# Attention and an eight-expert MoE on one core: the source of the clearing zeros, three chunks of expert 0, and expert 1's sums of x

## The chip, the cores and the metric

The kernel runs on one core of one Trainium2 chip. The metric is the device time of one execution in microseconds; the three timed runs of the kernel before gave 689.43, 690.41 and 692.71 us, with a median of 690.41 us. The engines are named as the profile names them: PE (TensorE; PEld is its weight load), DVE (VectorE), ACT (ScalarE), POOL (GpSimd) and SP (SyncE, which here only issues DMA transfers; SPq is its queue).

## The reference

Attention over 4 batches, 8 heads, 768 positions and 64 columns per head: each query sees the 31 keys within 16 positions and 24 block summaries (the maximum of 32 keys, the mean of 32 values). Its output, 3072 rows of 512, goes through a mixture of 8 experts; each row goes to the two with the highest noisy logits.

```python
x = np.ascontiguousarray(attn_out.transpose(0, 2, 1, 3)).reshape(B * S, H * D)   # 3072 x 512
logits = x @ w_gate
noise_scale = np.log1p(np.exp(x @ w_noise))
noisy_logits = logits + noise_scale * noise
top2 = np.argpartition(-noisy_logits, 2, axis=1)[:, :2]
...
for e in range(E):                      # 8
    for k in range(2):
        mask = top2[:, k] == e
        h = np.maximum(x[mask] @ w1[e], 0.0)                          # 512 -> 1024
        out[mask] += top2_w[mask, k, None] * (h @ w2[e])              # 1024 -> 512
```

## The kernel before

**Stages.** Attention runs over 24 row tiles of 128 rows and fills the first 145 us or so. Each finished tile of x is split into a high and a low half of fp16 (1024 columns together) and stored to a table `xd` in HBM; the gate is worked out beside it. A decoded table then holds, for every expert, the rows that it takes, in 816 slots: seven chunks, six of 128 rows and a last one of 48. The order of all instructions on each engine is that of the code (a manual schedule), so a waiting instruction holds up everything behind it on its engine.

**An expert's input.** `x_gather(e, c)` (L740) gathers the rows of a chunk from `xd` by an indirect DMA, issued on POOL, into one of four buffers `XG` taken in turn; the first three chunks of expert 1 go into the buffers `PREV` instead, which later hold earlier output rows. `x_trans(e, c)` (L754) transposes a chunk into `XTE[e]` by a DMA issued on SP (L758). `x_trans_pe` (L762) does the same by eight transposes on PE (L766) into a PSUM bank and one ACT copy out of it (L767); before, chunks 5 and 6 of expert 0 take that way.

**Weights.** `w_load(e, i)` (L621 for the four slices of w1, L624 for those of w2) brings a slice through one of four staging buffers `stg`; ACT and DVE split it into a high and a low half of fp16 (`w1_hi` L674, `w1_lo` L679, `w_hi`, `w_lo` L646). For experts 1 to 7 sums of blocks of w1 are made as well (`w1_sums`, DVE, L657 to L662).

**Expert 0's first layer** is plain: `mm1_pe` (L780), twelve matmuls for each of eight strips, in two halves. Half 0 is chunks 0 to 2, half 1 is chunks 3 to 6 and begins behind the second layer of chunks 0 to 2 (`mm2_high`, `mm2_low`, L931), between whose low passes the transposes on PE stand. `mm1_out` evicts a strip (ACT L790, DVE L791), and `y_out` scales a chunk's output on DVE (L952) and scatters it from POOL.

**Experts 1 to 7** use seven block products instead of eight for each of four strips, so 28 products (`mm1_all`, `product`, L816). Three of the x blocks and one of their combinations are sums: `t_diff` (POOL, L693) makes a difference of the high or of the low halves, `t_join` (DVE, L649) adds the two, and `t_two`, `t_four` (DVE), `t_hi` (ACT, L713) and `t_lo` (DVE, L649) make the four blocks and split them into fp16 (`tx`). `p` is an ACT copy of a product (L838), `c` a sum on DVE (L858), `htl` the low half of an evicted strip (L824).

**What sets the order.** For the preparation of expert e + 1 a table gives each step a tick within expert e: `put(e, k, f, ...)` and `steps` fill it, `step(e, k)` issues it. For experts 1 to 7 a tick is one product of the first layer (28 of them, `M2`) or one pass of the second (21). For expert 0 ticks 0 to 2 stand behind the low passes of chunks 0 to 2, ticks 3 to 10 behind the eight strips of half 1, the rest behind the passes of chunks 3 to 6. Ahead of that, `finish_table` (L1216) issues the gathers and loads that follow the gate. `clear` (L988) writes zeros to 384 rows of the output; it runs eight times, with the zeros read from `XG[3]`.

Of the kernel before, what the change touches and what calls it, by code (L numbers as in the profile page):

```python
# [8 lines left out]
F32 = mybir.dt.float32  # L9
# [5 lines left out]
OP = mybir.AluOpType  # L15
# [45 lines left out]
def attn_moe(ctx, tc, qt, kt, vt, wgn, noise, w1, w2, out):  # L61
    nc = tc.nc
# [32 lines left out]
    LAST = NCH - 1  # L95
# [180 lines left out]
    def bank():  # L276
        return banks[0].tile([P, 1, 512], F32, name="h")
# [339 lines left out]
    def w_load(e, i):  # L617
        s = stage.tile([P, SW], F32, name="stg")[:, :1024]
        SG[e, i] = s
        if i < 4:  # L620
            nc.sync.dma_start(s, w1[e, i * P:(i + 1) * P, :])  # L621
        else:
            i -= 4
            nc.sync.dma_start(s.rearrange("p (c d) -> p c d", c=2),  # L624
                              w2[e, 2 * i * P:2 * (i + 1) * P, :].rearrange("(c p) d -> p c d", p=P))
# [17 lines left out]
    def w_lo(e, i):  # L643
        n, sc = ("w1", W1S) if i < 4 else ("w2", W2S)
        hi, lo = [WT[e][n + x][:, i % 4, :] for x in "hl"]
        nc.vector.scalar_tensor_tensor(lo, SG[e, i], sc, hi, op0=OP.mult, op1=OP.subtract)  # L646

    def plus(o, a, b, op=OP.add):
        nc.vector.scalar_tensor_tensor(o, a, 1.0, b, op0=OP.mult, op1=op)  # L649
# [33 lines left out]
    def tt(e, j):  # L683
        TT[e, j] = side_pool[0].tile([P, 2, HC], F32, name=f"t{j}")
        return TT[e, j]

    def xb(e, j, k, low):
        return XTE[e][:, 4 * low + 2 * j:4 * low + 2 * j + 2, HC * k:HC * k + HC]

    def t_diff(e, j, low):  # L690
        i = (1, 1) if j == 3 else (0, 1)
        o = (0, 1) if j == 3 else (0, 0)
        nc.gpsimd.tensor_tensor(tt(e, 0 if low else j), xb(e, *i, low), xb(e, *o, low), op=OP.subtract)  # L693

    def t_join(e, j):
        plus(TT[e, j], TT[e, j], TT[e, 0])

# [56 lines left out]
    def x_trans(e, c):  # L754
        if c == 0:
            XTE[e] = (late[0] if e % 2 else moe).tile([P, 2 * DC, CAP], F16, name="xte")
        n = min(P, CAP - c * P)
        nc.sync.dma_start_transpose(out=XTE[e][:, :, c * P:c * P + n], in_=XC[e, c][:n])  # L758
# [3 lines left out]
    def x_trans_pe(e, c):  # L762
        n = min(P, CAP - c * P)
        pt = bank()[:, 0].bitcast(F16).rearrange("p (k n) -> p k n", k=2 * DC)
        for k in range(2 * DC):
            nc.tensor.transpose(pt[:, k, :n], XC[e, c][:n, k * P:(k + 1) * P], identh[:n, :n])  # L766
        nc.scalar.activation(XTE[e][:, :, c * P:c * P + n], pt[:, :, :n], AF.Copy)  # L767
# [18 lines left out]
    def mm1_out(e, half, f):  # L786
        c0, c1 = (0, H0) if half == 0 else (H0, CAP)
        ph = PH[f][:, :c1 - c0]
        hh, hl = HT
        nc.scalar.activation(hh[:, f, c0:c1], ph, AF.Relu)  # L790
        nc.vector.scalar_tensor_tensor(hl[:, f, c0:c1], ph, 0.0, hh[:, f, c0:c1], op0=OP.max, op1=OP.subtract)  # L791
# [149 lines left out]
    def mm2_low(e, c, pv):  # L941
        py = PY[c]
        mm2_pass(e, c, "w2l", HT[0], 2, py)
        y_out(e, c, pv)
# [197 lines left out]
    PREV = []  # L1142
    w1_alloc(1, True)
    for i in range(3):
        x = late[0].tile([P, DM], F32, name=f"prev{i}")
        PREV.append(x)

    spair.close()
# [24 lines left out]
    norm_lo(NT - 1, nc.vector)  # L1173
    x_out(NT - 1)
    for i in range(8):
        clear(XG[3].bitcast(F32), 3)
    for x in HT:
        nc.gpsimd.memset(x[:, :, CAP:], 0.0)
    for x in PREV:
        nc.gpsimd.memset(x, 0.0)  # L1180
    mm1_out(0, 0, 0)
    mm1_pe(0, 0, 1)
    mm1_pe(0, 0, 2, None, lambda: gate_c(5, og))
# [32 lines left out]
    def finish_table():  # L1216
        decode(TB.rearrange("p e c w -> p (e c) w"), 0, NS)
        last_ids()
        for c in range(3, NCH):
            x_gather(0, c)  # L1220
        for f in range(4, 8):
            w_lo(0, f)
        for c in range(3):
            x_gather(1, c)
        w_load(1, 0)
        w_load(1, 2)
        for c in range(3, LAST - 1):
            x_trans(0, c)
        w_load(1, 1)
        w_load(1, 3)  # L1230
        for c in range(3):
            x_trans(1, c)

    finish_table()
    mm2_high(0, 0)
# [10 lines left out]
    def put(e, k, f, *a):  # L1246
        plan.setdefault((e, k), []).append((f, a))
# [5 lines left out]
    def steps(e, where, at_):  # L1253
        for k, f, *a in at_:
            put(where, k, f, e, *a)

    for k, c in ((0, 3), (1, 4), (1, 5), (2, 6)):
        put(0, k, x_gather, 1, c)
        put(0, k, x_trans, 1, c)
    steps(1, 0, (  # L1260
        (1, w1_sums, 0, 0), (2, w1_sums, 0, 1), (2, w1_hi, 0, 0), (3, w1_lo, 0, 0), (3, w1_hi, 0, 1),
        (4, w1_lo, 0, 1, (0,)), (5, w1_lo, 0, 1, (1,)), (5, w1_sums, 1, 0), (6, w1_sums, 1, 1), (6, w1_hi, 1, 0),
        (7, w1_lo, 1, 0), (7, w1_hi, 1, 1), (8, w1_lo, 1, 1, (0,)), (8, t_diff, 3, 0), (8, t_diff, 3, 1),
        (9, w1_lo, 1, 1, (1,)), (9, t_diff, 1, 0), (11, t_join, 3), (11, t_diff, 1, 1), (11, t_alloc), (11, t_two, 0),
        (11, t_hi, 3), (12, t_two, 1), (12, t_hi, 2), (13, t_join, 1), (13, t_hi, 1), (14, t_lo, 3), (14, t_lo, 2),
        (15, t_four), (15, t_hi, 4), (16, t_lo, 1), (17, t_lo, 4)))
    for i, k in enumerate((13, 14, 18, 19)):
        put(0, k, w_load, 1, 4 + i)
    M2 = 7 * (FC // 2)

    def gathers(e, where, early, k):
        for c in range(4):
            put(where, early[c], x_gather, e, c)
            put(where, k, x_trans, e, c)
        for c in range(4, NCH):
            put(where, k + 2 * (c - 2), x_gather, e, c)
            put(where, k + 2 * (c - 2), x_trans, e, c)

    gathers(2, 0, (10, 10, 11, 11), 11)
    for e in range(1, E):  # L1280
        put(e, 0, w2_alloc, e)
        for i, (k0, k1) in enumerate(((3, 3), (8, 9), (15, 16), (22, 22))):
            put(e, k0, w_hi, e, 4 + i)
            put(e, k1, w_lo, e, 4 + i)
            if e + 1 < E:
                put(e, k1 + 1, w_load, e + 1, (0, 2, 1, 3)[i])
        if e + 1 == E:
            break
        n = e + 1
        put(e, 0, w1_alloc, n, True)  # L1290
        steps(n, e, (
            (1, t_diff, 3, 0), (4, t_diff, 3, 1), (10, t_join, 3),
            (7, t_diff, 1, 0), (11, t_diff, 1, 1), (17, t_join, 1)))
        steps(n, e, [(M2 + k, *a) for k, *a in (
            (0, t_alloc), (0, t_two, 0), (0, t_hi, 3), (1, t_two, 1), (1, t_hi, 1), (2, t_lo, 3), (2, t_hi, 2),
            (3, w1_sums, 0, 0), (3, w1_hi, 0, 0), (4, w1_sums, 0, 1), (5, t_lo, 2), (5, w1_hi, 0, 1),
            (6, w1_lo, 0, 0), (7, t_four), (8, w1_lo, 0, 1, (0,)), (8, t_hi, 4), (9, w1_lo, 0, 1, (1,)),
            (9, t_lo, 1), (10, w1_sums, 1, 0), (10, w1_hi, 1, 0), (11, w1_sums, 1, 1), (11, t_lo, 4),
            (12, w1_lo, 1, 0), (12, w1_hi, 1, 1), (13, w1_lo, 1, 1, (0,)), (14, w1_lo, 1, 1, (1,)))])
        for i, k in enumerate((9, 10, 14, 15)):  # L1300
            put(e, M2 + k, w_load, n, 4 + i)
        if e + 2 < E:
            gathers(e + 2, e, (8, 12, 16, 20), M2)

    for c in range(3):
        mm2_low(0, c, None)
        if c:
            x_trans_pe(0, LAST - 2 + c)
        step(0, c)
    late_tick = [3]  # L1310

# [132 lines left out]
```

## Time and profile before

| | |
|---|---|
| timed runs, us | 689.43, 690.41, 692.71 |
| profiled execution, us | 693.0 |
| its span, us | 691.1 |
| granted PE clock, mean over the span | 0.98 |
| PE busy, us | 643.7 (93% of the span) |
| DVE busy, us | 494.8 (72%) |
| ACT busy, us | 318.0 (46%) |
| POOL busy, us | 328.8 (48%) |
| DMA moved | 125.90 MB, 182 GB/s mean |

The span runs from the first to the last instruction of the profiled execution; 1.9 us of its time lie around it. The busy shares are averages over attention, expert 0 and the experts behind it, whose limits differ, so the views below are read stage by stage: the chain is followed back from the last instruction, and a row of the timeline carries in brackets how long its engine was idle ahead of it and whose end released it ("remote" where the trace shows no releaser on this core).

### The profile page before, as it was taken

How to read it: one execution, taken by the hardware profiler on the slowest of the kernel's cores; microseconds unless marked ns; L12 is line 12 of the kernel's file. 1: busy time of each engine (PE TensorE's matmuls, PEld its weight loads, DVE VectorE, ACT ScalarE, POOL GpSimd, SP SyncE). 2: the span in 40 equal slices, each digit the busy share in tenths (PEclk: the TensorE clock that was granted, in tenths of full speed). 3: DMA queues.
4: the chain of work that ended last, by engine and by line, in shares of the span. 5: the costliest groups of instructions: out<-in, count | busy, mean ns of one | idle time of the engine just before them, and what ended most of it. 6: DMA issues, size and time to landing. Idle time of an engine off the chain costs nothing.

```text
span 691.1 us, 14068 instructions
## 1 busy us (share of the span) xinstructions
PE 643.7 (93%) x5400; PEld 371.2 (54%) x5400; DVE 494.8 (72%) x901; ACT 318.0 (46%) x678; POOL 328.8 (48%) x463
## 2 busy tenths in 40 slices
PE   7998888979789989999999999999999999999992
PEld 6767666755344544465455545544654555455441
DVE  5758898879469577957877795879578677956410
ACT  2879788843052345235415632652364156326100
POOL 3454344520829483755556385627555551640131
PEclk9999999999989999999999999999999999999996
DMA  8999999759993946735672765567457622431020
GB/s 283 291 283 309 278 308 290 235 140 374 260 170 89 255 158 170 212 139 183 153 228 82 202 159 184 170 156 187 149 182 161 228 76 96 158 115 31 32 92 20
DMA packets 100297, 125.90 MB, mean 182 GB/s; under 512 B 58985, under 2 KB 63857, under 8 KB 100220
## 3 DMA queue, kind: packets, MB, share of 16 engines
q1 hardware_dynamic: 88076, 88.64, 45.1%
q0 software_dynamic: 12144, 36.28, 16.4%
q8 instruction: 44, 0.72, 0.4%
q14 instruction: 33, 0.27, 0.1%
HBM read 87.57 MB, written 26.21 MB: 165 GB/s over the span
## 4 chain that ended last, share of the span: by engine, by line
PE 76%; DVE 8%; ACT 5%; DMA 3%; another core or an unknown queue 3%; issue 2%; SPq 0%; POOL 0%; POOLq 0%; DVEq 0%
PE pt L931 34%; PE h L816 24%; PE a L816 4%; PE h L780 4%; PE pt L928 3%; ACT p L310 2%; PE s L296 2%; PE pt L316 2%; DMA hth<-in_vt_dram 1%; DMA q<-in_qt_dram 1%; PE o L329 1%; ACT pts L319 1%; DVE rh L541 1%; PE pt L241 1%
## 5 line engine op out<-in xcount | busy, mean ns | idle before, releaser
L92 POOL DMA_INDIRECT out_dram<-y,tb x48 | 64.1, 1335 | 159.9 <-DVE y L954 153.7
L931 PEld LDWEIGHTS <-hth 128*128 128x128 f16 x768 | 75.0, 98 | 89.3
L931 PE MATMUL pt<-w2h,htl 128*128 128x512 f16 x376 | 88.8, 379 | 0.0
L931 PE MATMUL pt<-w2h,hth 128*128 128x512 f16 x376 | 88.8, 379 | 0.0
L931 PE MATMUL pt<-w2l,hth 128*128 128x512 f16 x376 | 88.7, 379 | 0.0
L92 POOL DMA_INDIRECT xg<-xd,tb x53 | 69.4, 1309 | 38.1 <-DVE w2l L646 26.9
L816 PE MATMUL h<-tx,sh 128*128 128x408 f16 x336 | 79.5, 338 | 3.2 <-DVE htl L824 2.4
L693 POOL TENSOR_TENSOR t<-xte 128x816 f32<-128x816 f16 x28 | 50.5, 1830 | 46.6 <-DVE t L649 28.0
L954 DVE SCALAR_TENSOR_TENSOR y<-pt,tb,prev 128x512 f32<-128x512 f32 x42 | 31.4, 749 | 54.4 <-PE pt L931 54.4
L646 DVE SCALAR_TENSOR_TENSOR w2l<-stg,w2h 128x1024 f16<-128x1024 f32 x32 | 48.8, 1533 | 27.1 <-ACT w2h L629 22.9
L816 PEld LDWEIGHTS <-w1h 128*128 128x128 f16 x448 | 43.4, 98 | 35.9 <-issue 4.2
L931 PEld LDWEIGHTS <-htl 128*128 128x128 f16 x384 | 37.6, 98 | 45.3
L816 PE MATMUL h<-xte,w1h 128*128 128x408 f16 x224 | 57.5, 338 | 0.0
L92 POOL DMA_INDIRECT prev<-out_dram,tb x42 | 50.5, 1201 | 12.7 <-issue 12.7
L358 POOL TENSOR_TENSOR xr<-x,xr 128x512 f16<-128x512 f32 x22 | 25.4, 1157 | 64.6 <-ACT xr L351 36.6
L310 ACT ACTIVATE p<-s,nm 128x118 f32<-128x118 f32 x192 | 53.4, 377 | 0.8
L838 ACT ACTIVATE p<-h 128x408 f32<-128x408 f32 x28 | 14.3, 512 | 76.1 <-issue 65.5
L816 PEld LDWEIGHTS <-sh 128*128 128x128 f16 x336 | 33.0, 98 | 28.9 <-issue 4.1
L713 ACT ACTIVATE tx<-t 128x816 f16<-128x816 f32 x28 | 24.0, 880 | 49.1 <-DVE t L649 48.4
L821 ACT ACTIVATE hth<-h 128x408 f16<-128x408 f32 x56 | 27.7, 508 | 34.6 <-DVE h L852 33.3
L816 PE MATMUL h<-tx,sl 128*128 128x408 f16 x168 | 43.1, 338 | 0.0
L674 ACT ACTIVATE sh<-ws 128x1536 f16<-128x1536 f32 x14 | 20.8, 1482 | 37.7 <-DVE ws L649 33.7
(204 smaller groups left out, 1244.6 us busy)
## 6 DMA issues: line engine op xcount, KB each, us to landing
stg<-in_w_dram SPq DMA_DIRECT2D x64, 512.0 KB
hth<-in_vt_dram SPq DMA_DIRECT2D x8, 780.0 KB
vw<-in_vt_dram SPq DMA_DIRECT2D x32, 195.0 KB
q<-in_qt_dram SPq DMA_DIRECT2D x24, 256.0 KB
xd<-xr SPq DMA_DIRECT2D x24, 256.0 KB
out_dram<-xg SPq DMA_DIRECT2D x8, 768.0 KB
kb<-in_kt_dram SPq DMA_DIRECT2D x6, 768.0 KB
htl<-in_vt_dram SPq DMA_DIRECT2D x16, 195.0 KB
```

Source lines behind the costliest of these rows:

```text
L92: return nc.gpsimd.indirect_dma_start(**kw)
L310: nc.scalar.activation(PE_[t][:, a, hp, :], SC[t][:, a, hp, :], AF.Exp, bias=NM[t][:, 1, a, hp:hp + 1], scale=0.125)
L358: engine.tensor_tensor(XR[t][:, DM:], X[t], XR[t][:, 0:DM], op=OP.subtract)
L646: nc.vector.scalar_tensor_tensor(lo, SG[e, i], sc, hi, op0=OP.mult, op1=OP.subtract)
L674: nc.scalar.activation(h, x, AF.Copy, scale=W1S)
L693: nc.gpsimd.tensor_tensor(tt(e, 0 if low else j), xb(e, *i, low), xb(e, *o, low), op=OP.subtract)
L713: nc.scalar.activation(TX[e][:, 0, j - 1], t_of(e, j), AF.Copy)
L780: nc.tensor.matmul(ph[:, :n], w[wn][:, c, f * P:(f + 1) * P], x[:, xo + c, c0:c1], start=(k == 0), stop=(k == 11), skip_group_check=hook i ...
L816: nc.tensor.matmul(o, lhs[a][:, c], rhs[b][:, c], start=start and n == 0, stop=stop and n == 5, skip_group_check=True)
L821: nc.scalar.activation(HT[0][:, f, c0:c1], c, AF.Relu)
L931: nc.tensor.matmul(py, hx[:, f, c * P:c * P + P], w[:, f, :], start=first, stop=final, skip_group_check=True)
L954: nc.vector.scalar_tensor_tensor(y, py[:, :d], gw, pv[:, :d], op0=OP.mult, op1=OP.add)
```

## The change

1. **Zeros.** The eight clears read zeros from `PREV[2]`; the `PREV` buffers are set to zero where they are allocated, ahead of the pads of `HT` on POOL.
2. **Expert 0.** Chunks 4, 5 and 6 go through `x_trans_pe` (before: 5 and 6); the DMA transpose of chunk 4 is gone.
3. **Order in `finish_table`.** SP's queue alternates loads of w1 and transposes.
4. **Expert 1's sums of x.** A new function `t_all` takes the place of `t_diff` and `t_join`: three operations on DVE in place of two on POOL and one on DVE, twice. The steps on w1 and on x for expert 1 get other ticks.
5. **Later steps.** Loads of w2 for expert 1 go to ticks 14, 16, 18, 19 (before 13, 14, 18, 19), the gathers of the last three chunks of expert 2 two ticks earlier, and expert 2's differences and joins six ticks later within expert 1.

```diff
+    def t_all(e, j):
+        i = (1, 1) if j == 3 else (0, 1)
+        o = (0, 1) if j == 3 else (0, 0)
+        t = tt(e, j)
+        plus(t, xb(e, *i, 0), xb(e, *o, 0), OP.subtract)
+        plus(t, t, xb(e, *i, 1))
+        plus(t, t, xb(e, *o, 1), OP.subtract)
...
         x = late[0].tile([P, DM], F32, name=f"prev{i}")
+        nc.gpsimd.memset(x, 0.0)
         PREV.append(x)
...
     for i in range(8):
-        clear(XG[3].bitcast(F32), 3)
+        clear(PREV[2], 3)
     for x in HT:
         nc.gpsimd.memset(x[:, :, CAP:], 0.0)
-    for x in PREV:
-        nc.gpsimd.memset(x, 0.0)
...
         w_load(1, 0)
+        x_trans(0, 3)
         w_load(1, 2)
-        for c in range(3, LAST - 1):
-            x_trans(0, c)
+        x_trans(1, 0)
+        x_trans(1, 1)
         w_load(1, 1)
+        x_trans(1, 2)
         w_load(1, 3)
-        for c in range(3):
-            x_trans(1, c)
...
     steps(1, 0, (
...
-        (4, w1_lo, 0, 1, (0,)), (5, w1_lo, 0, 1, (1,)), (5, w1_sums, 1, 0), (6, w1_sums, 1, 1), (6, w1_hi, 1, 0),
...
+        (7, w1_hi, 1, 1), (8, w1_lo, 1, 0), (9, w1_lo, 1, 1, (0,)), (10, w1_lo, 1, 1, (1,)), (10, t_all, 3),
...
-    gathers(2, 0, (10, 10, 11, 11), 11)
+    gathers(2, 0, (10, 10, 11, 11), 11, (13, 15, 17))
...
+        d = 6 if e == 1 else 0
         steps(n, e, (
-            (1, t_diff, 3, 0), (4, t_diff, 3, 1), (10, t_join, 3),
-            (7, t_diff, 1, 0), (11, t_diff, 1, 1), (17, t_join, 1)))
+            (1 + d, t_diff, 3, 0), (4 + d, t_diff, 3, 1), (10 + d, t_join, 3),
+            (7 + d, t_diff, 1, 0), (11 + d, t_diff, 1, 1), (17 + d, t_join, 1)))
...
     for c in range(3):
         mm2_low(0, c, None)
-        if c:
-            x_trans_pe(0, LAST - 2 + c)
+        x_trans_pe(0, LAST - 2 + c)
         step(0, c)
```

**SP, from the clears to expert 1's first transposes.** Before (`xte_2739` is expert 0's transposed x, `xte_3341` expert 1's; `xg3` and `xg0` are buffers of `XG`; the four `stg` rows are slices 0, 2, 1, 3 of expert 1's w1):

```order
L991 DMA out_0_dram<-xg3_163 128x3x512 x8
L621 DMA stg_3331<-in_w1_dram 128x1024
L621 DMA stg_3333<-in_w1_dram 128x1024
L758 DMA_TRANSPOSE xte_2739<-xg3_163 128x8x128
L758 DMA_TRANSPOSE xte_2739<-xg0_160 128x8x128
L621 DMA stg_3337<-in_w1_dram 128x1024
L621 DMA stg_3339<-in_w1_dram 128x1024
L758 DMA_TRANSPOSE xte_3341<-prev0_2974 128x8x128
L758 DMA_TRANSPOSE xte_3341<-prev1_2975 128x8x128
L758 DMA_TRANSPOSE xte_3341<-prev2_2976 128x8x128
```

And now, at the same place (expert 1's transposed x is `xte_3336`; lines behind `t_all` have moved by eight):

```order
L999 DMA out_0_dram<-prev2_2978 128x3x512 x8
L621 DMA stg_3331<-in_w1_dram 128x1024
L766 DMA_TRANSPOSE xte_2739<-xg3_163 128x8x128
L621 DMA stg_3334<-in_w1_dram 128x1024
L766 DMA_TRANSPOSE xte_3336<-prev0_2974 128x8x128
L766 DMA_TRANSPOSE xte_3336<-prev1_2976 128x8x128
L621 DMA stg_3339<-in_w1_dram 128x1024
L766 DMA_TRANSPOSE xte_3336<-prev2_2978 128x8x128
L621 DMA stg_3342<-in_w1_dram 128x1024
```

Chunk 4's transpose (from `xg0`) is gone, chunk 3's stands one load earlier, and the last two loads of w1 stand behind two and three of expert 1's transposes.

**DVE, expert 1's sums of x, beside expert 0's second layer.** Before (`t3`, `t2`, `t1`, `t0` are sums, `tx` their fp16 halves, `y` a scaled output):

```order
L791 SCALAR_TENSOR_TENSOR htl_91<-h_3633,hth_90 128x432
L649 SCALAR_TENSOR_TENSOR t3_3611<-t3_3611,t0_3613 128x816
L649 SCALAR_TENSOR_TENSOR t2_3669<-t3_3611,xte_3341 128x816
L649 SCALAR_TENSOR_TENSOR t2_3669<-t2_3669,xte_3341 128x816
L952 TENSOR_SCALAR y_3703<-pt_3656,tb_178 128x512
L649 SCALAR_TENSOR_TENSOR t1_3631<-t1_3631,t0_3666 128x816
L649 SCALAR_TENSOR_TENSOR tx_3668<-t3_3611,tx_3668 128x816
```

And now:

```order
L799 SCALAR_TENSOR_TENSOR htl_91<-h_3635,hth_90 128x432
L679 SCALAR_TENSOR_TENSOR w1l1_2971<-ws_3578,w1h1_2970 128x512
L649 SCALAR_TENSOR_TENSOR t3_3651<-xte_3336 128x816
L649 SCALAR_TENSOR_TENSOR t3_3651<-t3_3651,xte_3336 128x816 x2
L649 SCALAR_TENSOR_TENSOR t2_3673<-t3_3651,xte_3336 128x816
L649 SCALAR_TENSOR_TENSOR t2_3673<-t2_3673,xte_3336 128x816
L960 TENSOR_SCALAR y_3707<-pt_3663,tb_178 128x512
L649 SCALAR_TENSOR_TENSOR t1_3713<-xte_3336 128x816
L649 SCALAR_TENSOR_TENSOR t1_3713<-t1_3713,xte_3336 128x816 x2
```

Each join has become three operations that read the transposed x itself, with no input from POOL; a residual of w1 now stands right ahead of them.

**DVE, expert 2's first join, inside expert 1's first layer.** Before (`h` and `c22` are sums of products, `t3_3882` and `t0_3914` expert 2's differences):

```order
L646 SCALAR_TENSOR_TENSOR w2l_3868<-stg_3724,w2h_3867 128x1024
L852 TENSOR_TENSOR h_3893<-h_3893,u2_3890 128x408
L649 SCALAR_TENSOR_TENSOR t3_3882<-t3_3882,t0_3914 128x816
L858 TENSOR_TENSOR c22_3987<-h_3960,u3_3985 128x408
L824 SCALAR_TENSOR_TENSOR htl_91<-h_3893,hth_90 128x408
```

And now, with the rows that have come ahead of it:

```order
L860 TENSOR_TENSOR h_3898<-h_3898,u2_3895 128x408
L866 TENSOR_TENSOR c22_3991<-h_3963,u3_3989 128x408
L832 SCALAR_TENSOR_TENSOR htl_91<-h_3898,hth_90 128x408
L850 TENSOR_TENSOR a_4008<-a_4008,p1_4001 128x408
L832 SCALAR_TENSOR_TENSOR htl_91<-c22_3991,hth_90 128x408
L832 SCALAR_TENSOR_TENSOR htl_91<-a_4008,hth_90 128x408
L832 SCALAR_TENSOR_TENSOR htl_91<-h_3919,hth_90 128x408
L646 SCALAR_TENSOR_TENSOR w2l_3875<-stg_3791,w2h_3874 128x1024
L649 SCALAR_TENSOR_TENSOR t3_3946<-t3_3946,t0_3981 128x816
L860 TENSOR_TENSOR h_3963<-h_3963,u2_3954 128x408
```

The join has moved behind the next residual of w2 and the sums and evictions that follow the waits for products.

More of the change, by code (lines that the diff above doesn't have):

```diff
@@ L1260, in attn_moe, with gathers @@
     steps(1, 0, (
-        (1, w1_sums, 0, 0), (2, w1_sums, 0, 1), (2, w1_hi, 0, 0), (3, w1_lo, 0, 0), (3, w1_hi, 0, 1),
-        (4, w1_lo, 0, 1, (0,)), (5, w1_lo, 0, 1, (1,)), (5, w1_sums, 1, 0), (6, w1_sums, 1, 1), (6, w1_hi, 1, 0),
[L1263 to L1267, printed above, removed]
+        (2, w1_hi, 0, 0), (3, w1_sums, 0, 0), (3, w1_sums, 0, 1), (3, w1_hi, 0, 1), (4, w1_lo, 0, 0),
+        (5, w1_lo, 0, 1, (0,)), (6, w1_lo, 0, 1, (1,)), (6, w1_sums, 1, 0), (6, w1_hi, 1, 0), (7, w1_sums, 1, 1),
+        (7, w1_hi, 1, 1), (8, w1_lo, 1, 0), (9, w1_lo, 1, 1, (0,)), (10, w1_lo, 1, 1, (1,)), (10, t_all, 3),
+        (11, t_alloc), (11, t_two, 0), (11, t_two, 1), (11, t_hi, 3), (11, t_hi, 2), (13, t_all, 1), (13, t_hi, 1),
+        (14, t_lo, 3), (14, t_lo, 2), (16, t_lo, 1), (16, t_four), (16, t_hi, 4), (19, t_lo, 4)))
+    for i, k in enumerate((14, 16, 18, 19)):
         put(0, k, w_load, 1, 4 + i)
     M2 = 7 * (FC // 2)
-    def gathers(e, where, early, k):
+    def gathers(e, where, early, k, then):
         for c in range(4):
@@ L1275, in gathers @@
         for c in range(4, NCH):
-            put(where, k + 2 * (c - 2), x_gather, e, c)
-            put(where, k + 2 * (c - 2), x_trans, e, c)
-    gathers(2, 0, (10, 10, 11, 11), 11)
+            put(where, then[c - 4], x_gather, e, c)
+            put(where, then[c - 4], x_trans, e, c)
+    gathers(2, 0, (10, 10, 11, 11), 11, (13, 15, 17))
     for e in range(1, E):
@@ L1302, in attn_moe @@
         if e + 2 < E:
-            gathers(e + 2, e, (8, 12, 16, 20), M2)
+            gathers(e + 2, e, (8, 12, 16, 20), M2, (M2 + 4, M2 + 6, M2 + 8))
     for c in range(3):
         mm2_low(0, c, None)
-        if c:
-            x_trans_pe(0, LAST - 2 + c)
+        x_trans_pe(0, LAST - 2 + c)
         step(0, c)
```

## The prediction

> **What bounds the kernel now.** I read the page first (PE busy for 93% of the span, PE 76% of the chain that ended last), then the chain in order of time where attention hands over to the experts (start us, length us, what):
>
> ```profile
> 162.76 5.86 PE h L780 x36
> ...
> 168.65 0.49 ACT hth L790
> ...
> 193.29 19.03 PE h L780 x96
> ...
> 230.60 1.14 PE h L816 x6
> ...
> 264.92 31.08 PE pt L931 x144
> ...
> 298.74 1.14 PE h L816 x6
> ...
> 328.09 1.94 PE pt L931 x9
> ```
>
> From 193.29 on the chain is almost all PE, so what PE loses there the whole span loses. Three places stand out. Ahead of 193.29 the chain leaves PE and runs over copies of transposed chunks of expert 0 (below). Expert 1's first layer takes 264.92 - 230.60 = 34.32 us; expert 2's, with as many products, 328.09 - 298.74 = 29.35 us: expert 1 loses 4.97 us. And the second half of expert 0's first layer takes 19.03 us. PE's own timeline (start, length, engine, line, operation; in brackets idle time ahead and what ended it):
>
> ```profile
> 182.86 0.61 PE L766 MATMUL h<-identh,xg 128*128 128x128 f16 x8
> 183.31 1.89 PE L931 MATMUL h<-w2l,hth 128*128 128x512 f16 x8
> 185.13 0.37 PE L766 MATMUL h<-identh,xg 48*128 48x48 f16 x8
> 193.29 1.60 PE L780 MATMUL h<-xte,w1h 128*128 128x432 f16 x4 [7.79 <-ACT xte L767]
> 198.29 1.62 PE L780 MATMUL h<-xte,w1h 128*128 128x432 f16 x8
> ...
> 200.48 1.62 PE L780 MATMUL h<-xte,w1h 128*128 128x432 f16 x8
> ...
> 233.66 0.51 PE L816 MATMUL h<-tx,sh 128*128 128x408 f16 x2 [0.88 <-ACT p L838]
> ...
> 250.67 0.84 PE L816 MATMUL h<-tx,sh 128*128 128x408 f16 x2 [2.36 <-DVE htl L824]
> ```
>
> PE stands still for 7.79 us, and then runs slowly: a strip of twelve matmuls takes 200.48 - 198.29 = 2.19 us, eight strips 17.5, but the 96 took 19.03, so 1.5 us are lost behind the gap. In expert 1 it waits 0.88 us at 233.66 and 2.36 at 250.67; the other 4.97 - 0.88 - 2.36 = 1.7 us go in slow matmuls, such as the pair of 0.84 us behind the longer wait, where the one at 233.66 took 0.51. The windows say the same of the clock (busy us of each engine, granted clock, DMA share, GB/s):
>
> ```profile
> 172.00:174.00 2.00, 2.00 (x11) 0.89 (x10) 2.00 (x3) 0.00 (x0) 0.41 (x1) 1.00 0.00 1
> 186.00:193.30 7.30, 0.01 (x1) 0.01 (x1) 0.64 (x1) 1.57 (x3) 4.06 (x8) 0.72 1.12 262
> 193.30:204.00 10.70, 10.70 (x52) 5.39 (x52) 7.77 (x12) 5.18 (x8) 2.25 (x3) 0.87 1.09 226
> ```
>
> The granted clock is 0.72 in the gap and 0.87 behind it. The DMA engines are idle at 172 to 174 (share 0.00) and full from 186 to 204 (above 1).
>
> **The change part by part.** *Chunk 4 on TensorE, and an earlier start of the gathers (term A).* Eight more transposes cost PE 183.31 - 182.86 = 0.45 us, and ACT one more copy of 1.02 us, which lies beside PE's next 1.89 us of products. One DMA transpose goes. On SP the second half then waits for chunk 3's transpose alone, issued first in this row:
>
> ```profile
> 179.33 2.63 SPq L758 DMA_TRANSPOSE xte<-xg  x2
> 173.59 1.67 POOL L92 DMA_INDIRECT xg<-xd,tb  x1 [26.92 <-DVE w2l L646]
> ```
>
> The first gather (second row) stands at the head of POOL's queue while DMA idles. The row names DVE, but its target is the buffer the eight clears read, and the DMA share is 0.00 at 172 to 174, when they are through; with zeros read from another buffer, what is left is the decoded table. By the idle 2 us I estimate it and the gathers behind it 1 to 2 us earlier, worth nothing by itself on PE but cover for chunk 4, which PE now wants at about 181 (182.86 less one pass of 1.89 us).
>
> What is left of the gap then? If PE's signals come as promptly as for the eviction at 168.65, 0.03 us behind the end of the matmuls it follows (162.76 + 5.86 = 168.62), the copy of the last chunk, 0.50 us, and 0.1 of issue remain: 7.79 - 0.6 - 0.45 = 6.7 us gained. But look at what released the copies:
>
> ```profile
> 188.19 1.02 ACT L767 ACTIVATE xte<-h 128x1024 f16<-128x1024 f16 x1 [19.06 <-remote]
> 192.75 0.49 ACT L767 ACTIVATE xte<-h 128x384 f16<-128x384 f16 x1 [3.53 <-remote]
> ```
>
> PE's rows of these chunks end at 183.47 (182.86 + 0.61) and 185.50 (185.13 + 0.37), yet ACT started 4.7 and 7.2 us later, released by something that the trace calls "remote", while DMA was full. If that lateness doesn't hang on the chunk taken off the DMA or on the two weight loads moved back, A is -1.0 (the added copy) to 0. I take 6.7, the end nearest to an ordinary hand-over between these engines, and keep -1.0.
>
> *The slow clock behind the gap (term B)* goes with the gap: 1.5 us, or 0 if it stays.
>
> *Expert 1's sums of x on VectorE, and expert 2's steps six ticks later (term C).* The wait at 250.67 starts on POOL:
>
> ```profile
> 206.07 6.79 POOL L693 TENSOR_TENSOR t<-xte 128x816 f32<-128x816 f16 x3 [9.91 <-DMA xte<-xg]
> 243.43 5.34 POOL L693 TENSOR_TENSOR t<-xte 128x816 f32<-128x816 f16 x3 [8.61 <-DMA xte<-xg]
> 247.12 2.51 DVE L649 SCALAR_TENSOR_TENSOR t<-t,t 128x816 f32<-128x816 f32 x1 [2.81 <-POOL t L693]
> 255.29 0.99 DVE L649 SCALAR_TENSOR_TENSOR t<-t,t 128x816 f32<-128x816 f32 x1
> ```
>
> Expert 2's join holds DVE from the start of its 2.81-us wait to 249.6; queued behind it are a sum and the residuals that free PE's banks. Now the join comes six products later (6 x 29.35 / 28 = 6.3 us, at expert 2's pace of 28 products), and POOL, rid of 6.79 us of expert 1's differences and one more, issues expert 2's gathers by that much earlier. Both exceed the 2.81 + 2.51, so the wait and its slow pairs go: 2.36 + 1.7 = 4.1 us. The 0.88 at 233.66 waits for an ACT copy and stays. The least is 0, were the wait to move to another product.
>
> [...]
>
> DVE pays: two joins become six operations of 0.99 us, +4.0 us. What hides it: DVE loses its contention with POOL, as between 2.51 and 0.99 for the same join; expert 1's last scaled rows were ready early:
>
> ```profile
> 226.59 1.91 DVE L649 SCALAR_TENSOR_TENSOR tx<-t,tx 128x816 f16<-128x816 f32 x2
> 204.02 1.57 ACT L674 ACTIVATE w1h<-stg 128x512 f16<-128x512 f32 x2
> 182.06 1.07 SPq L621 DMA_DIRECT2D stg<-in_w_dram  x2
> 184.45 11.34 SPq L758 DMA_TRANSPOSE xte<-prev  x3
> ```
>
> The scaled rows (first row) end at 228.5, 5.2 us ahead of the first product that reads any (233.66). A and B bring PE there 8.2 us sooner. If DVE's stretch moves with PE's strips, as the evictions and scaled outputs in it do, its extra 4.0 us fit into 5.2 and cost nothing; if it keeps its time, the rows come 8.2 + 4.0 - 5.2 = 7.0 us late. I take 0, nearer to a stretch that is mostly fed by PE, and keep 7.0 as the upper end.
>
> *Load order.* Loads of w1 slices 1 and 3 (issued 182.06) stand behind two and three transposes that wait for gathers; the third of these ended at 195.8 (184.45 + 11.34). Their first reader is ACT at 204.02, or 196 if all moves 8.2 us sooner. I cost the order at nothing, hidden by expert 0's strips; what it costs without that cover is R3 below. Earlier POOL memsets and the other zeros: the clears start behind the same stores, nothing.
>
> Sum: 6.7 + 1.5 + 4.1 = 12.3 us. The profiled execution took 693.0 us (span 691.1), 2.6 above the median of 690.41 and 0.3 above the slowest run. 693.0 - 12.3 = 680.7, 690.41 - 12.3 = 678.1; I forecast **680**.
>
> **The rivals.** *R1, the late signals stay*: whatever "remote" is, it lies in the traffic of 180 to 204, which the change shifts by a microsecond or two and shortens by one transpose of nine. For: DMA share above 1 there. Against: the loads that fill it are moved out. Then C less 1.0 for the copy: 690.4 - 4.1 + 1.0 = 687. *R2, VectorE becomes the bound*: half of that stretch keeps its time, expert 1's first layer waits 3.5 us for scaled rows and runs slowly behind it (1.7, as in expert 1 now): 680 + 5.2 = 685. Against: what DVE does there follows PE's strips. *R3, slower*: the loads of w1 slices 1 and 3 slip past their use. If both leave at 195.8 instead of 182.06, 13.7 us later, and their sums block DVE's queue, the rows end at 228.5 + 13.7 + 4.0 = 246.2 instead of 228.5, and the product of 233.66 comes 12.5 us later, whatever PE gained ahead of it; less C that is 690.4 + 8.4 = 699. It decides from a slip of about 5 us (13.7 - 8.4), below which the time is under that of before; against it speaks that the first of the two stands only behind transposes whose gathers start early. *R4, the change doesn't do what it says*: the first gather waited for the decoded table (the DVE that its row names) rather than for the clears, the second half waits as long for chunk 3, and expert 1's wait reappears two products on: 690.
>
> **How the numbers follow.** Forecast 0.55 (677 to 684), R1 0.18, R2 0.12, R4 0.07, R3 0.08. The range 675 to 689 takes in forecast, R1 and R2; its lower end is 678.1 less the 0.88 us, and 2 us for the spread of the runs; its upper end is R1 with those 1.7 us left. Half a per cent, 3.5 us, is about what can be told from no change. Faster by more than that (under 687.0): forecast, R2 and nearly half of R1, 0.74; within: 0.18; slower: 0.08.
>
> **What would show it.** PE's gap ahead of the first L780 strip (L788 then) under 1.5 us and the 96 matmuls in 17.6 us: A and B. If ACT's copies still start at 188 and 193 by "remote", R1. Expert 1's first layer near 30.3 us with no wait on DVE: C; a wait at the first product on the scaled rows: R2. ACT's first reading of slices 1 and 3 released by a DMA: R3. The prediction is wrong if the gap keeps its 7 us or PE's strips meet a new one.

## The result, and the profile after

The changed kernel took 679.56 us (median; runs of 679.25 to 683.04) against 689.92 (688.55 to 692.71) for the kernel before: a ratio of 0.9856, 95% interval 0.9811 to 0.9901. The forecast was 680.

The chain of waits of the kernel after, where attention hands over to the experts (start us, length us, what):

```profile
159.05 5.85 PE h L788 x36
...
182.82 2.22 PE h L788 x12
185.03 12.27 DMA stg<-in_w_dram
197.33 1.06 ACT w1h L674
...
222.29 1.14 PE h L824 x6
...
252.56 17.48 PE pt L939 x81
```

The first half of expert 0's first layer ends at 164.90 instead of 168.62, and expert 1's first product comes at 222.29 instead of 230.60. The releaser that the profile didn't know is gone. In its place a load of w1 (L621) stands on the chain for 12.27 us: the fourth slice, which now stands last in SP's queue. PE's own timeline of the same kernel (start, length, engine, line, operation; in brackets the idle time ahead and what ended it):

```profile
181.87 0.37 PE L774 MATMUL h<-identh,xg 48*128 48x48 f16 x8
182.82 0.89 PE L788 MATMUL h<-xte,w1h 128*128 128x432 f16 x4 [0.58 <-ACT xte L775]
...
202.55 1.25 PE L939 MATMUL pt<-w2h,hth 128*128 128x512 f16 x5 [1.40 <-ACT hth L798]
...
207.63 0.39 PE L939 MATMUL pt<-w2h,htl 128*128 128x512 f16 x1 [0.59 <-DVE htl L799]
...
213.98 1.89 PE L939 MATMUL pt<-w2h,hth 128*128 128x512 f16 x8 [0.78 <-DVE y L960]
...
244.12 0.51 PE L824 MATMUL h<-tx,w1h 128*128 128x408 f16 x2 [1.03 <-ACT u L864]
...
252.40 1.89 PE L939 MATMUL pt<-w2h,hth 128*128 128x512 f16 x8
```

The gap ahead of the second half is 0.58 us instead of 7.79. Behind the strips PE has new waits of 1.40, 0.59 and 0.78 us, all in the second layer of expert 0 and all behind ACT and DVE. Expert 1's first layer has one wait of 1.03 us and ends at 252.40. On POOL and ACT (same columns):

```profile
167.54 1.02 POOL L92 DMA_INDIRECT xg<-xd,tb  x1 [24.36 <-DVE oc L567]
182.28 0.49 ACT L775 ACTIVATE xte<-h 128x384 f16<-128x384 f16 x1 [1.01 <-PE h L774]
197.33 1.06 ACT L674 ACTIVATE w1h<-stg 128x1024 f16<-128x1024 f32 x1 [4.50 <-DMA stg<-in_w_dram]
```

The first gather is released by the table's own step (L567). It starts 2.6 us behind the end of expert 0's first half (167.54 - 164.90), before 5.0 us (173.59 - 168.62): 2.4 us earlier. The copy of the last chunk is released by PE's transposes, 0.04 us behind their end (181.87 + 0.37 = 182.24), no longer by "remote". And ACT waits 4.50 us for the fourth slice. In these two windows (busy us of each engine, granted clock, DMA share, GB/s) the granted clock is 1.00, and the 2 us from 172.00, in which the DMA share before was 0.00, now have 1.13:

```profile
172.00:174.00 2.00, 2.00 (x11) 0.93 (x10) 0.94 (x1) 0.00 (x0) 1.78 (x4) 1.00 1.13 316
183.00:193.00 10.00, 10.00 (x56) 5.38 (x55) 5.44 (x9) 5.65 (x9) 4.22 (x8) 1.00 1.05 243
```

To compare executions, PE's timeline is cut at six of its instructions: the end of the first half of expert 0's first layer (A), of the last transposes on PE (B), the first matmul of the second half (C), the first matmul of chunk 3's second layer (D), the first product of expert 1 (E), the first second-layer matmul of expert 1 (F). Stages in us, of the profiled execution of each kernel; the experiments follow below.

| kernel | start to A | A to B | gap B to C | strips C to D | second layer D to E | first layer of expert 1, E to F | F to the end |
|---|---|---|---|---|---|---|---|
| before | 168.6 | 16.9 | 7.8 | 18.9 | 18.4 | 34.2 | 426.4 |
| after | 164.9 | 17.3 | 0.6 | 17.5 | 21.9 | 30.2 | 425.1 |
| control (before again) | 171.5 | 16.9 | 7.0 | 19.1 | 20.1 | 36.6 | 426.6 |
| pe3 | 166.3 | 17.4 | 4.0 | 20.2 | 18.4 | 33.9 | 426.6 |
| zeros | 165.8 | 18.5 | 0.6 | 17.5 | 20.4 | 36.0 | 424.0 |
| experts | 167.4 | 16.9 | 8.0 | 20.1 | 20.2 | 30.2 | 424.5 |
| order | 167.6 | 16.9 | 7.6 | 19.7 | 18.4 | 34.2 | 426.3 |
| a_xg3 | 168.6 | 17.3 | 6.8 | 18.8 | 20.7 | 31.5 | 424.7 |
| a_dma4 | 168.7 | 16.9 | 3.2 | 19.2 | 20.6 | 30.2 | 425.1 |
| a_loads | 169.5 | 17.3 | 0.9 | 17.5 | 20.6 | 30.2 | 425.2 |
| after_c (after again) | 165.4 | 17.3 | 0.6 | 17.5 | 20.8 | 32.3 | 425.1 |
| zeros_exp | 168.2 | 17.6 | 2.6 | 17.5 | 20.6 | 31.5 | 425.4 |
| a_nod6 | 168.8 | 17.3 | 0.6 | 17.5 | 20.6 | 30.3 | 425.3 |
| best | 166.3 | 17.3 | 0.6 | 17.5 | 20.5 | 30.2 | 425.6 |

From before to after the two profiles differ by 691.1 - 677.5 = 13.6 us: -3.7 up to A, +0.4, -7.2, -1.4, +3.5, -4.0 and -1.3. The medians differ by 10.4 us. The stage up to A lies between 164.9 and 171.5 us whatever the kernel (before and control, the same kernel, have 168.6 and 171.5), so the 3.7 us there can't be put down to the change.

### The profile page after: what moved, and what is told of

Read it like the earlier page. It is cut to its first block, busy times and chain, and to the rows that moved or that the text cites. A ratio compares the mean times of both kernels' runs of the same rounds, so it can differ in the third digit from the quotient of the medians.

```text
span 677.5 us, 14084 instructions
## 1 busy us (share of the span) xinstructions
PE 639.6 (94%) x5408; PEld 368.5 (54%) x5408; DVE 492.7 (73%) x905; ACT 318.6 (47%) x679; POOL 319.3 (47%) x459
## 4 chain that ended last, share of the span: by engine, by line
PE 70%; DVE 11%; ACT 7%; DMA 6%; issue 3%; POOL 1%; SPq 0%; POOLq 0%; DVEq 0%; ACTq 0%
PE pt L939 34%; PE h L824 21%; PE a L824 4%; PE pt L936 3%; DMA stg<-in_w_dram 2%; ACT p L310 2%; DMA hth<-in_vt_dram 1%; DMA q<-in_qt_dram 1%; PE h L788 1%; PE s L296 1%; PE pt L316 1%; DVE rh L541 1%; DVE t L649 1%; ACT pts L319 1%; ACT w2h L629 1%
## 5 line engine op out<-in xcount | busy, mean ns | idle before, releaser
L92 POOL DMA_INDIRECT xg<-xd,tb x53 | 68.0, 1282 | 46.2 <-DVE oc L567 24.8
L962 DVE SCALAR_TENSOR_TENSOR y<-pt,tb,prev 128x512 f32<-128x512 f32 x42 | 31.5, 749 | 53.9 <-PE pt L939 53.9
L824 PEld LDWEIGHTS <-w1h 128*128 128x128 f16 x448 | 43.2, 98 | 36.6 <-issue 4.7
L693 POOL TENSOR_TENSOR t<-xte 128x816 f32<-128x816 f16 x24 | 41.5, 1755 | 34.5 <-DVE t L649 29.9
L674 ACT ACTIVATE sh<-ws 128x1536 f16<-128x1536 f32 x14 | 20.8, 1483 | 41.0 <-DVE ws L649 33.0
```

What stands on the lines that cost most here:

```text
L92: return nc.gpsimd.indirect_dma_start(**kw)
L674: nc.scalar.activation(h, x, AF.Copy, scale=W1S)
L824: nc.tensor.matmul(o, lhs[a][:, c], rhs[b][:, c], start=start and n == 0, stop=stop and n == 5, skip_group_check=True)
L962: nc.vector.scalar_tensor_tensor(y, py[:, :d], gw, pv[:, :d], op0=OP.mult, op1=OP.add)
```

## The experiments

Three groups of four; each kernel is timed against runs of the kernel before taken beside it. The median of before was 695.62 us in the first group, 694.27 in the second and 693.78 in the third, 4 to 6 us above the 689.92 of the result, so ratios are compared and not times. In the third group the runs of before lie between 684.50 and 695.40 us, and its intervals are wide.

**control**: the kernel before, unchanged.

> The kernel before, unchanged, profiled once more. Theory G (the gap ahead of the second half of expert 0's first layer belongs to the kernel): 690 us +-2, PE's gap ahead of the first L780 strip again 6 to 9 us, the 96 matmuls behind it again over 18.5 us, the wait for expert 2's join in expert 1's first layer again some 2.4 us. Rival F (the gap belongs to the one profiled execution, which took 693.0 us against a median of 690): the same 690 us, but a gap under 3 us in this profile; then most of the change's 10 us must come from somewhere else.

696.02 us, ratio 1.0019 (0.9988 to 1.005); not the 690 expected, but neither were the runs of before beside it. The gap is there again. PE's and ACT's timelines of control:

```profile
188.06 0.37 PE L766 MATMUL h<-identh,xg 48*128 48x48 f16 x8
195.38 1.60 PE L780 MATMUL h<-xte,w1h 128*128 128x432 f16 x4 [6.96 <-ACT xte L767]
...
231.83 1.06 PE L928 MATMUL pt<-w2h,hth 128*64 128x256 f16 x16 [1.62 <-DVE y L952]
...
240.67 0.84 PE L816 MATMUL h<-tx,sh 128*128 128x408 f16 x2 [3.85 <-ACT p L838]
...
193.93 1.40 ACT L767 ACTIVATE xte<-h 128x1024 f16<-128x1024 f16 x2 [21.87 <-remote]
240.11 0.51 ACT L838 ACTIVATE p<-h 128x408 f32<-128x408 f32 x1 [8.08 <-remote]
```

Both transposed chunks are copied together at 193.93, 5.5 us behind the end of the second (188.06 + 0.37 = 188.43). And a second such lateness falls into expert 1's first layer: the copy `p` starts at 240.11, 4.3 us behind the end of the product that it copies (235.79); ACT had been idle for 8.08 us. The first profile of before doesn't show it: there the wait was for the join. So the gap belongs to the kernel, but where ACT starts late behind PE, and by how much, differs from one execution to the next. The second layer of expert 0 takes 20.1 us here, with a wait of 1.62 us behind a scaled output `y`; in the first profile of the same kernel it took 18.4.

**pe3**: the three chunks on TensorE alone.

```diff
-        for c in range(3, LAST - 1):
-            x_trans(0, c)
+        x_trans(0, 3)
...
-        if c:
-            x_trans_pe(0, LAST - 2 + c)
+        x_trans_pe(0, LAST - 2 + c)
```

> Before, with chunk 4 of expert 0 on TensorE as well (three chunks), and nothing else. Theory P (the gap hangs on chunk 4's DMA transpose): the gap falls under 1.5 us, the 96 matmuls to 17.6 us, the time to 690 - 6.7 - 1.5 = 682. Rival T (it hangs on the crowd of loads and transposes, or on chunk 3, which stays on the DMA): the gap stays over 5 us, 689 to 691.

691.83 us, 0.9946 (0.992 to 0.9971): 3.8 us, not 8. PE, ACT and POOL:

```profile
187.65 1.60 PE L780 MATMUL h<-xte,w1h 128*128 128x432 f16 x4 [3.97 <-ACT xte L767]
186.19 1.41 ACT L767 ACTIVATE xte<-h 128x1024 f16<-128x1024 f16 x2 [3.69 <-remote]
171.32 1.66 POOL L92 DMA_INDIRECT xg<-xd,tb  x1 [26.73 <-DVE w2l L646]
```

The last two copies start together at 186.19, again by "remote", 2.5 us behind the end of the last transposes (183.31 + 0.37 = 183.68). Neither theory's numbers were met; the gap doesn't hang on chunk 4's transpose alone.

**zeros**: the zeros from the third `PREV` buffer alone.

```diff
         x = late[0].tile([P, DM], F32, name=f"prev{i}")
+        nc.gpsimd.memset(x, 0.0)
...
-        clear(XG[3].bitcast(F32), 3)
+        clear(PREV[2], 3)
...
-    for x in PREV:
-        nc.gpsimd.memset(x, 0.0)
```

> Before, with the clears' zeros read from the third PREV buffer, and nothing else. If the first gather of expert 0 waits for the clears, it now starts within 1 us of the decoded table, some 5 us earlier than before; chunk 4 then lands about as much earlier. Theory P: the gap shrinks by 3 to 5 us, 685 to 687. Rival T (the crowd decides): the gap keeps 5 us or more, 689 to 691. If the gather waited for the table itself, it starts as before, and nothing moves.

684.99 us, 0.9868 (0.9826 to 0.9911): the ratio can't be told from that of the whole change (0.9856). POOL, PE and ACT:

```profile
168.40 1.02 POOL L92 DMA_INDIRECT xg<-xd,tb  x1 [24.37 <-DVE oc L567]
181.61 0.62 PE L766 MATMUL h<-identh,xg 128*128 128x128 f16 x8 [1.43 <-DMA xg<-xd,tb]
184.83 0.89 PE L780 MATMUL h<-xte,w1h 128*128 128x432 f16 x4 [0.58 <-ACT xte L767]
184.29 0.49 ACT L767 ACTIVATE xte<-h 128x384 f16<-128x384 f16 x1 [1.00 <-issue]
229.39 0.51 ACT L850 ACTIVATE u<-h 128x408 f32<-128x408 f32 x1 [1.73 <-remote]
229.96 0.51 PE L816 MATMUL h<-tx,sh 128*128 128x408 f16 x2 [2.19 <-ACT u L850]
```

The gather is released by the table and starts 2.6 us behind A, not 5.0, so only 2.4 us earlier where 5 were expected; still gap and slow strips are gone, though chunk 4 is still transposed by DMA. PE waits 1.43 us for a gathered chunk instead. Expert 1's first layer stays slow, 36.0 us, but not for the join: its longest wait, 2.19 us, is for a copy `u` that ACT starts by "remote". So an early gather doesn't end the late starts everywhere.

**experts**: the expert part alone: `t_all`, the new ticks of expert 1's steps and loads, the gathers and the six ticks, as in the change's diff.

```diff
-        (7, w1_lo, 1, 0), (7, w1_hi, 1, 1), (8, w1_lo, 1, 1, (0,)), (8, t_diff, 3, 0), (8, t_diff, 3, 1),
...
+        (7, w1_hi, 1, 1), (8, w1_lo, 1, 0), (9, w1_lo, 1, 1, (0,)), (10, w1_lo, 1, 1, (1,)), (10, t_all, 3),
...
-    gathers(2, 0, (10, 10, 11, 11), 11)
+    gathers(2, 0, (10, 10, 11, 11), 11, (13, 15, 17))
...
+        d = 6 if e == 1 else 0
```

> Before, with the expert part alone: expert 1's sums of x by three operations each on VectorE, the new ticks of expert 1's steps and loads, the earlier late gathers, and expert 2's differences and joins six ticks later. Theory C (term C of 4.1 us stands by itself): no wait of 2 us on the join in expert 1's first layer, which takes 30.2 to 30.5 us instead of 34.3; 686. Rival V (VectorE pays for it): expert 0's second layer gets waits of 3 us or more behind VectorE, 689 or more.

688.99 us, 0.9916 (0.9882 to 0.9949). The gap stays at 7.98 us; expert 1's first layer falls to 30.2 us; expert 0's second layer takes 20.2 us instead of 18.4. Theory C's 4.1 us and a part of rival V both show.

**order**: SP's new order alone, with chunk 4 by DMA behind chunk 3.

```diff
         w_load(1, 0)
+        x_trans(0, 3)
+        x_trans(0, 4)
         w_load(1, 2)
-        for c in range(3, LAST - 1):
-            x_trans(0, c)
+        x_trans(1, 0)
+        x_trans(1, 1)
         w_load(1, 1)
+        x_trans(1, 2)
         w_load(1, 3)
-        for c in range(3):
-            x_trans(1, c)
```

> Before, with the new order of loads and transposes in SP's queue alone (chunk 4 stays on the DMA, behind chunk 3; the zeros stay in XG[3]). Theory Z: the gathers still start late, so the gap stays over 5 us; within 3 us of before. Rival T (the crowd of loads makes the gap): the gap shrinks by 4 us or more, 685 or less.

693.83 us, 0.9982 (0.9951 to 1.0014), with a gap of 7.60 us: the order of loads does nothing by itself that can be measured.

**a_xg3**: after, with the zeros from `XG[3]` again.

```diff
-        clear(PREV[2], 3)
+        clear(XG[3].bitcast(F32), 3)
```

> After, with the clears reading their zeros from XG[3] again, so that the first gather waits for them as before; chunk 4 stays on TensorE. Theory Z (the early start of the gathers is what closes the gap): the first gather starts 4 to 6 us later, a gap of some 4 us comes back ahead of the second half of expert 0's first layer, with copies of ACT released late, and the strips slow down to 19 or 20 us: 685 to 687. Rival P (chunk 4 on TensorE closes it, with the new order of loads): gap under 1.5 us, strips 17.5, within 2 us of after.

690.08 us, 0.9925 (0.9893 to 0.9958). POOL, ACT and PE:

```profile
173.62 1.67 POOL L92 DMA_INDIRECT xg<-xd,tb  x1 [27.16 <-DVE w2l L646]
189.16 1.02 ACT L775 ACTIVATE xte<-h 128x1024 f16<-128x1024 f16 x1 [6.33 <-remote]
192.74 1.60 PE L788 MATMUL h<-xte,w1h 128*128 128x432 f16 x4 [6.78 <-ACT xte L775]
```

With one buffer's name put back, the gather is late again (5.0 us behind A), ACT's copy of chunk 5 starts 5.2 us behind the end of its transposes (183.33 + 0.61 = 183.94) by "remote", and a gap of 6.78 us is back, although chunk 4 is on TensorE and the loads have their new order.

**a_dma4**: after, with chunk 4 by DMA again.

```diff
         x_trans(0, 3)
+        x_trans(0, 4)
...
-        x_trans_pe(0, LAST - 2 + c)
+        if c:
+            x_trans_pe(0, LAST - 2 + c)
```

> After, with chunk 4 of expert 0 transposed by DMA again, behind chunk 3. Theory Z: the gap stays under 2 us, since the gathers start early; PE is rid of 0.45 us; 679 to 682. Rival P: the gap comes back with 4 us or more and slow strips: 685 or more.

687.36 us, 0.9897 (0.9858 to 0.9936). ACT and PE:

```profile
188.22 0.49 ACT L775 ACTIVATE xte<-h 128x384 f16<-128x384 f16 x1 [2.59 <-remote]
188.76 0.89 PE L788 MATMUL h<-xte,w1h 128*128 128x432 f16 x4 [3.22 <-ACT xte L775]
```

The gap of 3.22 us lies between the two theories; the strips, 19.2 us, are slow as rival P had it. The gather starts 2.6 us behind A here as in after, and yet the last copy starts 2.7 us behind the end of its transposes (185.17 + 0.37 = 185.54) by "remote": with chunk 4 on the DMA, the early start alone doesn't always close the gap.

**a_loads**: after, with all loads of expert 1's w1 ahead of its transposes.

```diff
         w_load(1, 2)
-        x_trans(1, 0)
-        x_trans(1, 1)
         w_load(1, 1)
-        x_trans(1, 2)
         w_load(1, 3)
+        for c in range(3):
+            x_trans(1, c)
```

> After, with all four loads of expert 1's w1 ahead of expert 1's first transposes. Theory L (the 3.5 us that expert 0's second layer lost in after come from slice 3's late load, for which ACT waited 4.5 us at 197.33, with VectorE's queue behind it): no such wait, the second layer's stretch falls from 21.9 to 18.4 us: 676. Rival D (VectorE's added sums are what PE waits for): the stretch keeps 21 us or more: 679 to 680. Rival T (loads ahead of the transposes bring the crowd back): a gap of 4 us ahead of the second half, 685.

685.77 us, 0.9884 (0.9834 to 0.9934). No DMA ends a wait of ACT among the strips any more, and PE's wait of 1.40 us is one of 0.16; yet the second layer's stretch takes 20.6 us, not 18.4. The time can't be told from that of after (0.9856 and, below, 0.9874, in other groups). Theory L holds for 1.3 us of the 3.5 at most.

**after_c**: after, unchanged.

> After, unchanged, timed and profiled once more beside the others of this call. Expected: gap of 0.6 us, strips 17.5, expert 1's first layer 30.2 us as in the first profile; the time 10 to 14 us under before on the same chip. If the gap's going were a matter of one lucky execution, the gap would show 3 us or more here.

681.78 us, 0.9874 (0.9786 to 0.9961). The gap is 0.58 us again. The wait for the fourth slice has shrunk by itself (ACT's 4.50 us are 3.40, PE waits 0.30 us where it waited 1.40), and expert 1's first layer has two waits of 1.82 and 1.14 us for ACT's copies `u` (L864).

**zeros_exp**: before, with zeros and the expert part, and neither chunk 4 on TensorE nor the new order. The diff is those of zeros and experts together.

> Before, with the zeros from the third PREV buffer and the expert part; chunk 4 stays on the DMA and SP's order is the old one. Theory Z (the early gathers close the gap, the expert part its own wait, the other two parts add nothing): gap under 2 us, expert 1's first layer 30.2 us, within 1.5 us of after. Rival P (chunk 4 on TensorE or the new order are needed as well): gap of 3 us or more, or a new wait for chunk 4; over 3 us above after.

681.63 us, 0.9845 (0.975 to 0.994): the time of after_c. Nor can this ratio be told from that of zeros alone (0.9868), although the expert part alone gave 0.9916: the times don't show what it adds to the zeros. PE's timeline of zeros_exp:

```profile
183.06 0.62 PE L774 MATMUL h<-identh,xg 128*128 128x128 f16 x8 [0.49 <-DMA xg<-xd,tb]
188.27 0.91 PE L788 MATMUL h<-xte,w1h 128*128 128x432 f16 x4 [2.56 <-DMA xte<-xg]
```

Here the gap of 2.56 us is a wait for chunk 4's DMA transpose. Such a wait is what the copy on TensorE spares once the gathers are early: 2.6 us less 0.6 in this execution, and nothing in zeros, whose gap is 0.6 with the same DMA transpose; in the median it doesn't show.

**a_nod6**: after, without the shift by six ticks.

```diff
-        d = 6 if e == 1 else 0
+        d = 0
```

> After, with expert 2's differences and joins at the ticks of before (not six later) within expert 1. Theory C1 (the shift of six products is what takes the wait off PE): expert 1's first layer gets a wait of 2 us or more on the join again and takes 33 us or more; 3 us or more above after. Rival C2 (POOL, rid of expert 1's differences, is early enough by itself): 30.2 to 30.8 us, the time of after.

681.11 us, 0.9859 (0.9765 to 0.9953), expert 1's first layer 30.3 us: rival C2. The shift does nothing that can be measured. POOL's row of expert 2's differences:

```profile
232.83 6.42 POOL L693 TENSOR_TENSOR t<-xte 128x816 f32<-128x816 f16 x3 [3.74 <-DMA xte<-xg]
```

They start 8.0 us behind E (232.83 - 224.84), before 12.9 (243.43 - 230.53), both times released by a transpose; the join at 238.08 doesn't wait for POOL.

**best**: after, with the loads as in a_loads and two operations of DVE moved (and the ACT step `t_hi` behind one of them).

```diff
-        (7, w1_hi, 1, 1), (8, w1_lo, 1, 0), (9, w1_lo, 1, 1, (0,)), (10, w1_lo, 1, 1, (1,)), (10, t_all, 3),
-        (11, t_alloc), (11, t_two, 0), (11, t_two, 1), (11, t_hi, 3), (11, t_hi, 2), (13, t_all, 1), (13, t_hi, 1),
+        (7, w1_hi, 1, 1), (8, w1_lo, 1, 0), (10, w1_lo, 1, 1, (1,)), (10, t_all, 3),
+        (11, t_alloc), (11, t_two, 0), (11, t_hi, 3), (13, w1_lo, 1, 1, (0,)), (13, t_two, 1), (13, t_hi, 2), (13, t_all, 1), (13, t_hi, 1),
```

> After, with all four loads of expert 1's w1 ahead of its first transposes, and on VectorE the residual of three sums of w1 (1.75 us) moved behind the strips and one of the sums of x (1.0 us) behind the first scaled output. If PE's waits in expert 0's second layer come from the order on VectorE (0.59 us on a low half, 0.78 us on a scaled output), they shrink by 1 to 1.5 us and the stretch falls from 21.9 to 19.5 us: 2 us under after. If VectorE is simply full there, the waits move on to the next output: within 1 us of after.

679.00 us (677.15 to 679.74), 0.982 (0.9731 to 0.9908), against 680.81 to 682.76 for after_c in the same group: the four runs of each don't overlap. But the stretch that was to shrink takes 20.5 us against after_c's 20.8. PE's timeline and DVE's:

```profile
219.46 1.06 PE L936 MATMUL pt<-w2h,hth 128*64 128x256 f16 x16 [1.74 <-DVE y L960]
206.52 1.00 DVE L649 SCALAR_TENSOR_TENSOR t<-xte 128x816 f32<-128x816 f16 x1
207.56 3.10 DVE L649 SCALAR_TENSOR_TENSOR t<-t,xte 128x816 f32<-128x816 f32 x3
210.57 0.74 DVE L960 TENSOR_SCALAR y<-pt,tb 128x512 f32<-128x512 f32 x1
211.23 1.75 DVE L679 SCALAR_TENSOR_TENSOR sl<-ws,sh 128x1536 f16<-128x1536 f32 x1
```

The three waits have become one of 1.74 us at the last chunk. DVE's rows stand back to back there, with no idle time ahead of any from 203.16 to 220.23, so it is full, and this order of its work only moved the wait. The 2.8 us between the medians aren't explained: the two profiles differ most in expert 1's first layer, 32.3 us in after_c against 30.2, where the edit changes nothing.

## Why the prediction came out right, and where it was wrong

**Term A, 6.7 us**: the size was right (gap -7.2, eight more transposes +0.4: 6.8), the cause was not. The failed step is "worth nothing by itself on PE but cover for chunk 4": the early start of the gathers is worth most of the gap. All six executions whose first gather waits for the clears (it starts 5.0 us behind A in each) have a gap of 4.0 to 8.0 us. Of the eight with the early gather (2.6 us behind A in each) five have 0.58 and one 0.91; the other two, 2.6 and 3.2, have chunk 4 on the DMA, as zeros (0.58) has too, so chunk 4 on TensorE guards what the early start gains. Chunk 4 on TensorE alone leaves 4.0 us (pe3), and 6.8 with the whole rest of the change (a_xg3). R1 placed the lateness in the traffic of 180 to 204; that it moves with the start of the gathers fits this, but what in the traffic does it isn't shown, and gathers delayed by other means than the clears weren't run. That the change shifts the traffic too little was wrong: 2.4 us, a little above the 1 to 2 us estimated, were enough.

**Term B, 1.5 us**: right, 18.9 to 17.5, in every execution whose gap was 2.6 us or less; not in the others.

**Term C, 4.1 us**: the size was right (34.2 to 30.2), half of the reason wasn't needed. The prediction counted both the six ticks and POOL's relief; without the six ticks the layer is as short (a_nod6), and expert 2's differences start 4.9 us earlier against E than before, where the prediction had POOL earlier by 6.79 us and more. Whether that is POOL's relief or the earlier gathers of expert 2 was not separated. Control and zeros add that in some executions this layer loses its time to copies that start late by "remote" (PE waits 3.85 us for `p` in control, 2.19 for `u` in zeros) instead of the join.

**VectorE and the order of loads, costed at 0**: wrong by 3.5 us in the first profile, by 2.1 to 2.4 in the others of the same kind (20.5 to 20.8 us for a stretch of 18.4). The step "its extra 4.0 us fit into 5.2" looked at the last scaled rows, which did come in time; it passed over the low halves and scaled outputs of expert 0, which stand between the other operations on the same queue and for which PE waits at once. That is R2's mechanism, a stage earlier than R2 put it. But the added sums are not its only cause: zeros and control, where POOL still makes the differences, have 20.4 and 20.1 us there, each with a wait for a scaled output. How much of the 2.1 to 2.4 us the sums cost is not shown; the expert part alone (experts) has 20.2 beside 18.4 in before, pe3 and order. R3's mechanism came in small: the fourth slice was late, ACT waited 4.50 us and PE 1.40, which is 0.16 with the loads put first (a_loads); but in after_c it was 0.30 and in a_nod6 nothing with the order unchanged, so the 1.40 belong in part to one execution.

**The sum**: -6.8 - 1.4 - 4.0 + 3.5 = -8.7 us in the stages that the prediction spoke of, against -12.3 predicted; with the 1.3 us behind F, which weren't foreseen and aren't explained, -10.0, near the 10.4 between the medians. That 680 was met is in part luck: the sum was taken from the profiled execution as well as from the median, and that execution stood 2.6 us higher, which made up for the cost left out.

## What to carry to other kernels

A buffer that is only read, by a slow store, held back the first write of the next stage here: in control the clears' last store, out of `XG[3]`, stands on the chain from 165.65 to 175.51, and the first gather behind it; the gather started 5.0 us behind A with the zeros in `XG[3]` and 2.6 with the zeros in `PREV[2]`. Look at what the head of a queue waits for while DMA is idle (share 0.00 from 172 to 174 in before), and give the slow reader a buffer nobody else needs soon. One edit of that kind can give as much as the larger change around it (zeros 0.9868, the whole change 0.9856); run the parts alone, and take them back one by one, before the credit is given. When work moves to an engine, check every output that stands in its queue among the new operations, not only the product of the new ones: in after PE waited 0.59 us for a low half and 0.78 for a scaled output.

## What the runs showed of the hardware

**Copies that start late behind PE.** In the kernel before, PE's transposes and products end, and the engines that read them start 4.7 us (ACT, 188.19), 7.2 us (ACT, 192.75) and 7.5 us (DVE's scaled output at 192.66, behind products that end at 185.20) later, with "remote" as the releaser, while the DMA share is 1.07 from 180 to 186 and 1.12 from 186.00 to 193.30; in control ACT starts 5.5 us late at 193.93 and 4.3 us late at 240.11, with a share of 0.97 from 236.00 to 240.60. The traces show the late start; that it is a signal of PE that comes late is not shown, and what makes the start late stays open. A share above 1 is no sufficient condition: after has 1.05 from 183 to 193 and no such wait. Whether transposes, gathers or loads do it was not separated, nor whether it is there when nothing is profiled.

**The clock behind short waits.** The windows of four kernels (busy us of each engine, granted clock in the third-last column), each from within 1.3 us of the end of a wait of PE. Before, behind 2.36 us:

```profile
250.70:252.00 1.30, 1.30 (x5) 0.55 (x5) 1.30 (x2) 0.86 (x4) 1.30 (x1) 0.50 0.50 120
```

zeros, behind 2.19 us:

```profile
230.00:232.00 2.00, 2.00 (x9) 0.95 (x9) 1.12 (x1) 1.32 (x2) 0.00 (x0) 0.67 1.13 246
```

a_dma4, behind 3.22 us:

```profile
190.00:192.00 2.00, 2.00 (x7) 0.91 (x6) 0.00 (x0) 0.17 (x1) 1.22 (x4) 0.50 1.14 349
```

zeros_exp, behind 2.56 us:

```profile
188.20:190.00 1.80, 1.73 (x10) 0.97 (x11) 0.00 (x0) 0.00 (x0) 1.03 (x2) 1.00 1.01 403
```

The clock fell to a half behind waits of 2.19, 2.36 and 3.22 us (0.67 in zeros is a mean over a window in which it fell: the pairs of matmuls take 0.51 us at 229.96 and 0.89 at 231.28), and not behind one of 2.56, where it is 1.00 up to 192.00: in these four the length of the wait alone doesn't decide, and what else does isn't shown.
